# One unit's second product by seven block products for eight, two copies moved to ScalarE, one group of products in two steps, and a new hand-written order

## The chip, the cores and the metric

The kernel runs on one core of one Trainium2 chip. The metric is the device time of one execution in microseconds (us), lower is better. The core's engines work side by side, each through its own queue and in its own order: TensorE (PE in the profile; its weight loads are PEld), VectorE (DVE), ScalarE (ACT), GpSimd (POOL) and SyncE (SP, which here only issues DMAs). All arithmetic is in float32.

## The reference, cut to what matters

`x` is 8 batches x 8 heads x 512 tokens x 64, `state` is 8 x 8 x 32 x 64; `w_in` is 512 x 2048 and `w_out` 2048 x 512, both handed over as float64.

```
a  = softmax(x @ state^T / 8)        # over the 32 states
xread = a @ state
a2 = softmax(state @ x^T / 8)        # over the 512 tokens
sread = a2 @ x
rows = concat([xread, sread]) laid out as (8 * 544) x 512
h = rows @ w_in
out = (h * erf(softplus(h))) @ w_out
```

## The kernel before, in words

**Units.** Attention's result for the tokens of a batch is never formed: `a` (kept as `y`) is multiplied by state @ w_in instead (function `mixed`, steps `A1m`, `A2m` and so on). The hidden dimension is done in two halves, A and B. A *unit* is one batch in one half: A1 to A7, then B0 to B7; SA and SB are the state rows of all batches. The first unit, batch 0 in half A, has a function of its own, `first_unit`, as everything waits for it at the start: its steps are named `n..` (mixed), `h..` (first product and activation) and `o..` (second product).

**Products by sevens.** All other units form a product of two matrices cut in 2 x 2 blocks from seven block products in place of eight, with sums and differences of blocks made by VectorE before (Strassen-Winograd). `hidden` does so for the first product (steps `A1f01` to `A1f17`, matmuls at line 704); `second` (line 767) does it once for a second product (steps `..p1` to `..p7` with four matmuls of 128 x 256 for each half, line 757), `second_twice` does it within each of the seven again (line 827). The four differences of `w_out` that they need are the steps `T1` to `T4`, VectorE, 128 x 1024 each.

**The first unit.** `first_unit` (line 967) makes eight hidden blocks k = 0 to 7: two steps of matmuls (`hkL`, `hkR`, line 987), softplus by ScalarE (`hks`), a copy of h by VectorE (`hkc`, line 1000), erf for two blocks at a time by ScalarE (`h0e`, `h2e`, `h4e`, `h6e`) and the product with h by VectorE (`h0g` to `h6g`). The second product is plain: for each of four row blocks, eight matmuls of 128 x 512 into one PSUM bank (line 1009, 16 steps `o00` to `o36` of two matmuls each), then one copy by ScalarE (`o0c`) and one store (`o0d`). Its steps lie scattered among those of A1 and A2.

**What sets the order.** Every piece of work is a named step. The string `ORDER` (lines 23 to 179) is a hand-written list of all 2,532 step names; `in_order` (line 1149) chains each engine's instructions in just that order, so no engine ever takes a later step while an earlier one waits. `~7*3` stands for three matmuls that compute nothing, which keep TensorE running.

**The start.** The tokens of batch 0 are turned on TensorE (`x00` to `x31`), then come scores in two parts (`t0`, `t1`), and for each part VectorE and ScalarE do the softmax: `max`, `less`, `exp`, `sum`, `inv`, `norm` (line 244), TensorE turns the result (`ta0`, `ta1`), and ScalarE copies it to `y` (`ta0c`, `ta1c`), which `h0L` and `h1L` read. Meanwhile the float64 words of `w_in` and `w_out` arrive in pieces and are converted: `i0a0`, `i0a1` on ScalarE, `i0v0` and `i0v1` on VectorE or GpSimd (lines 379 to 385), and likewise for `i1` to `o3`. `a1..` and `a2..` are the attention of the next batches, mostly on VectorE.

**ScalarE's tables.** Softplus, exp and erf are in different function tables here; the compiler puts a table load ahead of the first instruction that needs another one. The built program has 60.

Of the kernel before, what the change touches and what calls it, by code (L numbers as in the profile page):

```python
# [23 lines left out]
warm lx1 own lx2 lst0 lx3 lx0 i0l0 i0l1 i1l1 i1l0 i2l1 x10 s0 x10c x30 s0c0 x11 x30c s0c1 x20 x00  # L24
x20c x31 i2l0 x00c x21 x31c t0 s0c i0a0 x11c i3l1 i0a1 i0v0 i0v1 i0+a0 x01 i3l0 max0 x21c x01c
i0+a1 less0 ~7*2 t1 i0+v0 ls1 exp0 i0+v1 sum0 i1a0 o0l1 n00 max1 o0l0 q0 i1a1 inv0 q1 less1 norm0
exp1 n01 a1xq6 i1v0 q1c ~7*1 ta0 n01c0 sum1 a1xq7 n01c1 ta0c inv1 n00c1 n00c0 norm1 i2a0 ~7*3 h1L
i1v1 ta1 i2a1 i2v0 h0L ta1c q0c i2v1 i3a1 n02 big1 ub h0R a1xq3 n02c1 i3a0 big0 h1R a1xq2 ubc
n02c0 big i3v0 wt0 n10 h1c a1xq0 h3L i3v1 wt1 n10c1 h2L o1l1 o0a0 h0c a1xq5 a1tx3 h3R n10c0 o0a1
a1xq1 wz h2R wn0 n12 wn1 a1xq4 h5L n12c1 y01 h3s tw1 o1l0 o0v0 n12c0 o3l0 h0s y02 tw0 h2c o3l1 h1s  # L30
o2l1 tw1c h3c h5R o2l0 tw0c a1tx1 o0v1 h2s h6L h5c rd0 a1tx2 a1tx0 h0e h7L rn0 y04 h2e h0g rt0 yl0
h7R a1x3 rc0 o1a0 h6R h2g a1s o1a1 o1v0 h6c h4L o1v1 a1c1 a2xq7 h7c a1c0 h4R a1my1 a2xq5 o00 a1tu0
a1tu1 h7s hold a2xq6 a1mx0 h5s lst7 A1m h6s a1mx1 a1x2 lst2 a1sb0 lst1 a1sb1 lst3 a1x0 a1ex0 o20
a1my0 lst6 a2xq3 a1ex1 a1sm0 lst5 A1m11 a1sm1 A1m10 lst8 o02 A1m00 a1iz A1M1 A1m01 lst4 a2xq0 o2a1
a1nm0 o22 a1nm1 o2a0 a2xq4 a1ta0 a1ta1 a1ey0 A1f01 t0k y11 A1M2 A1f05 A1f0c y12 y13 a1ey1 A1f06
a1ty0 o3a0 a1ty1 A1f02 A1M3 a1kz A1f0u2 u0 y14 a2xq2 o3a1 A1M4 A1f07 a1iy a1x1 o3v0 A1f0c11 u1
A1f0u3 u0c o3v1 A1f11 a2xq1 A1f0c22 A1f04 u1c h4c h4s A1f03 A1f0c21 t01 A1f0s22 o10 T1 A1f1c a1z0
a1z2 t02 a1z3 o2v0 A1f16 a1z1 yk1 h4e A1f0c12 o2v1 A1f12 yl1 a2tx2 t3k A1f1u2 A1f15 h6e a2tx0
A1f17 A1f1c11 o12 T2 A1f1u3 t61 A1f1c22 rd1 A1f0s21 t41 A1f0s11 h4g A1f14 rn11 a2x0 rn10 rt1 y03
A1f13 h6g rc1 A1f1s11 a2s A1f0s12 T4 o04 a2c1 a3xq4 t21 a2c0 A1f1c12 A1f1c21 a3xq3 a2tu0 A1f1s22  # L40
o14 a3xq1 A1f1s21 t31 A1f1s12 a2mx0 a3xq6 o24 yk0 a2my0 a2sb0 a3xq5 A1e0 o26 a3xq2 A1e1 A1g0 o06
a3xq0 t1k a3xq7 o16 A1g1 a2x3 a2ex0 A2m a2ey0 a2sm0 o0c a2ey1 o0d o30 t32 t4k A2m10 a2iz a3tx0
a2x2 a2nm0 A2m11 A2m00 o32 a3tx2 A2M1 o34 a2ta0 a2ty1 A2f01 y21 a2ty0 o36 A2f0c A2M2 a2kz A2m01
y22 t2k t11 a2x1 A2f06 y24 A2M3 A2f02 t12 A2f0u2 y23 o3c A1q A2f05 A2f0c11 o2c A2f07 A2M4 A1ap50
t04 A2f0u3 T3 A2f11 a2z0 a2z3 A2f0c22 A2f04 a2z1 a2iy a2z2 A1A1 A1ap10 yl2 A2f0c21 o2d A2f1c A2f03
t22 o3d t42 o1c A1A2 A2f16 o1d t5k A2f12 t51 A2f1u2 A1A4 A1ap11 A2f0c12 A2f17 A2f0s22 t33 A2f1c11
rd2 t23 t13 A2f1u3 t34 A2f1s11 t52 A2f14 A1A3 rn20 rn21 A2f0s21 rt2 A1ap51 rc2 A1a2 A1ac A2f0s11
a3s t62 A1a3 A1ap60 a3c1 a4xq6 a3c0 A1ap61 A1b2 a3x1 a4xq1 A1ap20 t03 A1au2 t44 A2f0s12 a3tu0
a4xq2 A2f15 A1ap70 t14 a3mx0 a4xq0 A1ap71 t6k A2f1c22 A1ap21 a3sb0 A1au3 a4xq3 a3my0 A2f13 A1ac11
A1ap40 A1ac22 A1a4 A1bp10 a3ex0 A1bp11 t24 a3ey0 A1ap30 a3sm0 A2f1c21 A1ap41 a3ey1 a3iz A2f1c12  # L50
a3nm0 A1ap31 a4tx0 A3m A2f1s12 A1ac12 A1ac21 t43 A1bc a3ta0 A1d2 A1bp50 A1d3 A3m00 a3x3 A3m10
A1bp60 y31 A2f1s21 a3ty0 A1bp61 t53 A1bp51 A1b3 A1bu2 A3f01 A3m11 t63 A3m01 A1bp20 a3ty1 A2f1s22
A3M1 A3f0c a3kz A1bp70 t64 a4xq4 A3M3 A1bp71 A1bp21 y32 a3x2 t54 A2e0 A3f05 A1b4+ A3M2 A3f02 A1b4
a3x0 A3f06 A1bu3 y34 a4xq7 y33 A1bc22 A1bp40 A3f0u2 A2g0 A2e1 A1bp41 a3z3 A3f07 a3z0 a3z2 A1bp30
a3z1 A3f0u3 A3M4 A1d0 A3f0c11 A1bp31 yk2 A3f0c22 A3f04 a4xq5 A1bc12 A3f11 A2g1 A3f0c21 A1bc11
A3f03 A1bc21 A3f1c A1d1 A2ap10 A2q A3f16 A3f0s11 A1D0 rd3 a3iy A3f0c12 A3f1u2 A2A1 A3f17 rn31 a4x1
rn30 A3f0s12 a4x0 rt3 a4tx2 A3f0s21 A3f15 rc3 A3f1u3 A2ap50 A1D1 A2A2 A3f14 yl3 A3f1c22 A3f12 A2A4
A3f1c21 A2ap11 A3f1c11 A2a2 a4s A2ac A3f1s11 A2A3 A2ap20 a4c1 a5xq4 a4c0 A1U2 A2ap60 a5xq3 a4tu0
A1D4 A2ap61 a5xq2 A2a3 A3f13 A2au2 a5xq0 A3f1s22 A2ap21 A2b2 A3f0s22 a4x2 A2ap70 a5xq1 A2ac11
a4mx0 A3f1s12 A2ap71 a5xq6 A3f1c12 a4sb0 A2ap51 A2au3 a4my0 A3f1s21 A2bp10 A2bp11 A2a4 A2ap40  # L60
a4ey1 a5xq5 A2ap41 A1U3 a4ex0 A2b3 A1D2 A4m a4ey0 A2ac22 A1D3 A2ac21 a4sm0 A2bc A2ap30 A4m11 a4iy
a4iz A4m00 a5tx0 A2ap31 a4nm0 A4m10 A2bp60 A2ac12 A2bp61 A3e0 A2bp50 A4M1 a4ta0 A2bp51 A2bp20
A2b4+ y41 A2bp21 a4ty0 A4f01 A2bu2 A4m01 y42 A4M2 A2bp70 A4f0c a4ty1 A3e1 A2bp71 y44 A4f06 a4kz
y43 A2d3 A2b4 A4f05 a5xq7 A4M3 A2bu3 A4f0u2 A4f02 A2bc22 A2d0 A3g0 yl4 A2bp30 A4f0c11 A2bc11 A4f07
# [122 lines left out]
def kernel(  # L187
# [8 lines left out]
    nc = tc.nc  # L196
# [3 lines left out]
    P = 128  # L200
# [994 lines left out]
```

## Time and profile before

| | us |
|---|---|
| three runs: median (lowest to highest) | 682.49 (682.04 to 684.77) |
| the profiled execution, its own time | 681.77 |
| the profiled execution, span from first to last instruction | 680.0 |
| TensorE busy in the span | 673.0 |
| VectorE busy | 582.7 |
| ScalarE busy | 483.7 |
| granted TensorE clock, mean | 1.000 of full |

A float32 matmul of 128 x 128 x N is recorded as two instructions, so counts at lines 704, 757, 827 and 1009 are twice the number of matmuls. The duration of one instruction in the records overlaps with the next one's; what one more instruction costs its engine is the distance from start to start. By the waits of TensorE, it was held up four times by a named wait in the whole span, for 3.0 us in total, all before 35 us:

```profile
PE b L444 <- DMA big<-in_x_dram: 1.1, 2, 0.8
PE b L456 <- ACT big L250: 0.8, 1, 0.8
PE b L431 <- PEq L1179: 0.8, 1, 0.8
PE b L549 <- DVE sn L250: 0.3, 1, 0.3
```

### The profile page before, as it was taken

How to read it: one execution, taken by the hardware profiler on the slowest of the kernel's cores; microseconds unless marked ns; L12 is line 12 of the kernel's file. 1: busy time of each engine (PE TensorE's matmuls, PEld its weight loads, DVE VectorE, ACT ScalarE, POOL GpSimd, SP SyncE). 2: the span in 40 equal slices, each digit the busy share in tenths (PEclk: the TensorE clock that was granted, in tenths of full speed). 3: DMA queues.
4: the chain of work that ended last, by engine and by line, in shares of the span. 5: the costliest groups of instructions: out<-in, count | busy, mean ns of one | idle time of the engine just before them, and what ended most of it. 6: DMA issues, size and time to landing. Idle time of an engine off the chain costs nothing.

```text
span 680.0 us, 13845 instructions
## 1 busy us (share of the span) xinstructions
PE 673.0 (99%) x5578; PEld 589.3 (87%) x5578; DVE 582.7 (86%) x763; ACT 483.7 (71%) x758; POOL 125.1 (18%) x103
## 2 busy tenths in 40 slices
PE   8999999999999999999999999999999999999997
PEld 7756488988888898999998889899989898989996
DVE  5999899999989999998896689897966797878795
ACT  5998867877695877766886975767595768575831
POOL 0442202122232214020201013011111110201122
PEclk9999999999999999999999999999999999999999
DMA  9896753896796885784966355133232224141347
GB/s 296 199 271 182 154 163 78 215 165 159 148 189 127 186 213 102 209 191 119 224 214 163 87 129 100 26 59 60 32 79 38 43 30 116 20 67 17 46 89 123
DMA packets 145840, 87.16 MB, mean 128 GB/s; under 512 B 92784, under 2 KB 138096, under 8 KB 145776
## 3 DMA queue, kind: packets, MB, share of 16 engines
q1 hardware_dynamic: 126720, 67.78, 36.1%
q0 software_dynamic: 18512, 17.96, 21.1%
q8 instruction: 44, 0.72, 0.4%
q10 hardware_dynamic: 544, 0.52, 0.2%
q14 instruction: 20, 0.16, 0.1%
HBM read 46.14 MB, written 40.11 MB: 127 GB/s over the span
## 4 chain that ended last, share of the span: by engine, by line
PE 97%; DMA 1%; ACT 1%; issue 0%; SPq 0%; DVE 0%; ACTq 0%; DVEq 0%
PE b L827 47%; PE b L704 26%; PE b L1009 4%; PE b L655 4%; PE b L1049 4%; PE b L757 4%; PE b L987 2%; PE b L925 2%; PE b L539 1%; DMA big<-in_moe_w_in_dram 1%; PE b L564 1%; PE b L976 0%; PE b L456 0%; PE b L469 0%; PE b L463 0%
## 5 line engine op out<-in xcount | busy, mean ns | idle before, releaser
L735 POOL DMA_DIRECT2D out_dram<-res x67 | 80.0, 1337 | 425.9 <-DVE res L242 193.9
L827 PE MATMUL b<-big,ring 128*128 128x128 f32 x1196 | 150.3, 276 | 0.0
L827 PEld LDWEIGHTS b<-big,ring 128*128 128x128 f32 x1196 | 144.4, 192 | 6.7 <-issue 2.5
L250 ACT COPY ring<-b 128x512 f32<-128x512 f32 (+1 forms) x136 | 78.1, 584 | 89.5 <-PE b L704 69.4
L704 PE MATMUL b<-y,m 128*128 128x256 f32 x480 | 122.0, 381 | 0.1
L250 ACT COPY res<-b 128x512 f32<-128x512 f32 (+2 forms) x126 | 64.7, 521 | 47.8 <-PE b L827 38.3
L704 PEld LDWEIGHTS b<-y,m 128*128 128x128 f32 x480 | 86.2, 191 | 11.0 <-issue 1.0
L704 PE MATMUL b<-sy,m 128*128 128x256 f32 x360 | 91.4, 381 | 0.0
L244 DVE TENSOR_TENSOR ring<-ring 128x2048 f32<-128x2048 f32 (+1 forms) x36 | 77.6, 2168 | 8.2 <-ACT ring L712 6.1
L693 ACT ACTIVATE ring<-ring 128x512 f32<-128x512 f32 x128 | 77.9, 634 | 2.2 <-DVE ring L242 1.7
L704 PEld LDWEIGHTS b<-sy,m 128*128 128x128 f32 x360 | 65.3, 190 | 9.2 <-ACT b L250 0.8
L827 PEld LDWEIGHTS b<-ta,ring 128*128 128x128 f32 x548 | 68.0, 192 | 5.3 <-ACT b L250 1.7
L827 PE MATMUL b<-ta,ring 128*128 128x128 f32 x548 | 72.3, 276 | 0.0
L242 DVE TENSOR_TENSOR ring<-ring,b 128x512 f32<-128x512 f32 (+1 forms) x72 | 47.3, 660 | 28.5 <-PE b L704 15.7
L243 DVE TENSOR_TENSOR ring<-ring 128x1024 f32<-128x1024 f32 (+3 forms) x66 | 70.5, 1073 | 0.2
L827 PE MATMUL b<-big,ta 128*128 128x128 f32 x572 | 70.7, 275 | 0.0
L827 PEld LDWEIGHTS b<-big,ta 128*128 128x128 f32 x572 | 67.8, 192 | 1.3 <-ACT b L250 0.8
L242 DVE TENSOR_TENSOR res<-res,b 128x512 f32<-128x512 f32 (+2 forms) x60 | 36.1, 601 | 29.8 <-PE b L827 17.6
L712 ACT ACTIVATE ring<-ring 128x2048 f32<-128x2048 f32 x30 | 57.2, 1912 | 0.2
L250 ACT COPY b<-b 128x512 f32<-128x512 f32 (+2 forms) x63 | 34.6, 551 | 23.7 <-PE b L704 10.8
L242 DVE TENSOR_TENSOR res<-res 128x512 f32<-128x512 f32 (+1 forms) x56 | 42.1, 753 | 1.7 <-ACT res L250 0.8
L242 DVE TENSOR_TENSOR ring<-ring 128x1024 f32<-128x1024 f32 (+1 forms) x35 | 39.8, 1142 | 0.2
(153 smaller groups left out, 989.8 us busy)
## 6 DMA issues: line engine op xcount, KB each, us to landing
out_dram<-res POOLq DMA_DIRECT2D x63, 256.0 KB, 5.5
out_dram<-res SPq DMA_DIRECT2D x32, 256.0 KB, 3.4
big<-in_x_dram SPq DMA_DIRECT2D x30, 256.0 KB, 4.8
big<-in_x_dram SPq DMA_DIRECT2D x112, 64.0 KB, 3.1
big<-in_moe_w_in_dram SPq DMA_DIRECT2D x12, 512.0 KB, 7.1
big<-in_moe_w_out_dram SPq DMA_DIRECT2D x12, 512.0 KB, 4.7
kept_y<-y SPq DMA_DIRECT2D x8, 512.0 KB, 3.9
y<-kept_y SPq DMA_DIRECT2D x8, 512.0 KB, 4.3
```

Of the source, the lines that this page charges most:

```text
L242: add = lambda o, a, b: tt(o, a, b, op=ALU.add)
L243: sub = lambda o, a, b: tt(o, a, b, op=ALU.subtract)
L244: mul = lambda o, a, b: tt(o, a, b, op=ALU.mult)
L250: do[name] = lambda: f(*args)
L655: pe.matmul(out=to[j][e][q, :], lhsT=by, rhs=w_in[r, 4 * j:4 * j + 4, i, :], start=True, stop=True)
L693: act.activation(out=o, in_=i, func=ACTF.Softplus)
L704: pe.matmul(out=to[:, i], lhsT=xs[n - 1][:, q:q + P], rhs=ys[n - 1], start=(start and i == 0), stop=(i == 1), skip_group_check=True)
L712: step(u + "e%d" % o, lambda s=s: act.activation(out=s, in_=s, func=ACTF.Erf))
L735: nc.gpsimd.dma_start(out=to, in_=of, accum_op=ALU.add)
L757: pe.matmul(out=to[:, E2 * h:E2 * h + E2], lhsT=a[:, k // 2, k % 2], rhs=rhs[n][:, k], start=(start and h == 0 and k == 0), stop=(k == 3), ...
L827: pe.matmul(out=out_[:, P * j:P * j + P], lhsT=lhs[:, i], rhs=rhs[:, i], start=(start and j == 0 and i == 0), stop=(i == 1), skip_group_ch ...
L1009: pe.matmul(out=bank[3 + r % 3], lhsT=s[:, k, P * r:P * r + P], rhs=wo[0].w[:, k, :], start=(k == 0), stop=(k == NT - 1))
```

## The change

1. The second product of the first unit is done by `second`, now called A0: seven block products of 2 x 4 matmuls of 128 x 256 (56 in all) in place of 32 of 128 x 512. VectorE makes four sums of its blocks (`A0A1` to `A0A4`, 128 x 1024 each); ScalarE takes five results out of PSUM (`A0pc`, `A0pu2`, `A0pc11`, `A0pu3`, `A0pc21`) and VectorE two (`A0pc22`, `A0pc12`), where ScalarE took four. Four stores of the same size go out, cut by quarters and not by rows. `T1` to `T4` must now come before this product's parts, not after the plain product's last read of `w_out`.
2. The copies `h6c` and `h7c` go from VectorE to ScalarE.
3. `A1m` (line 649) becomes `A1m0` and `A1m1`, eight matmuls of 128 x 512 each.
4. `ORDER` is new from its start to about two thirds of its length; its last 783 names, from `B0ap30` on, are the same. Fillers of nothing in the start go from six matmuls to eleven. The compiled program now has 63 table loads, three more: one net in the work of A1 and A2, two in that of A7. Up to the copy `A1f0u2` (the second result that product A1 takes out of PSUM) it has six, where it had five.

```diff
-        def product():
-            for j in range(2):
+        def product(*js):
+            for j in js:
...
-        step(u + "m", product)
+        if u == "A1":
+            for j in range(2):
+                step("A1m%d" % j, product, j)
+        else:
+            step(u + "m", product, 0, 1)
...
-    def second(u, w, slot, nh, store):
+    def second(u, w, lhs, nh, store):
...
-                step("h%dc" % k, dve.tensor_copy, hs[:, k], to)
+                step("h%dc" % k, act.copy if k > 5 else dve.tensor_copy, hs[:, k], to)
...
-        def product(r, ks):
-            for k in ks:
-                pe.matmul(out=bank[3 + r % 3], lhsT=s[:, k, P * r:P * r + P],
-                          rhs=wo[0].w[:, k, :], start=(k == 0), stop=(k == NT - 1))
...
+        (A11, A12), (A21, A22) = ([s[:, 4 * k:4 * k + 4, 256 * r:256 * r + 256] for k in range(2)]
+                                  for r in range(2))
+        S1, S2, S3, S4 = (hs[:, 4 * (k // 2):4 * (k // 2) + 4, 256 * (k % 2):256 * (k % 2) + 256]
+                          for k in range(4))
+        step("A0A1", add, S1, A21, A22)
+        step("A0A2", sub, S2, S1, A11)
+        step("A0A3", sub, S3, A11, A21)
+        step("A0A4", sub, S4, A12, S2)
+        xs = (A11, A12, S4, A22, S1, S2, S3)
+        return lambda n, h, k: xs[n - 1][:, k, P * h:P * h + P]
...
-    seconds0()
     for n, f in enumerate(wo[0].sums()):
         step("T%d" % (n + 1), f)
+    second("A0", wo[0], lhs0, 2, lambda r, c, of: put(
+        rows_of(0)[:, 2 * r:2 * r + 2, E2 * c:E2 * c + E2],
+        of.rearrange("p (h e) -> p h e", h=2), False))
```

The new order around the start and the first unit (of the changed kernel; `...` leaves out names):

```
... x31 x11c x31c x21 x11c i0+a0 t0 i3l1 i0+a1 i0+v0 x21c i0+v1 i0a1 i3l0 t1 i0a0 max0 i0v0 less0
ls1 o0l1 i0v1 q0 exp0 max1 i1a0 q1 sum0 n00 i1a1 less1 a1xq2 inv0 i1v0 ~7*3 n01 n00c0 o0l0 exp1
norm0 i2a0 sum1 a1xq3 ~7*5 ta0 n00c1 q1c inv1 norm1 n01c0 ta0c i2v0 i2a1 ~7*3 ta1 i1v1 h0L ta1c ...
n02 ub h0R ... h1L ... h1R ...
... yl0 A1m0 a1mx0 h6s a2xq0 hold a1sb1 lst1 A0p10 ... A0p11 h7c ... A1m1 h6c ... A1f01 y11 ...
A1f07 ... A1f17 rn11 a2x3 rn10 t0k rt1 T2 A0p20 rc1 A0A1 ... A0p50 ... A0p60 ... A0d2
```

More of the change, by code (lines that the diff above doesn't have):

```diff
@@ L23 @@
 ORDER = """
[L24 to L52, printed above, removed]
@@ new lines @@
+s0c1 x20 x10c x31 i2l0 x20c x11 x31c x21 x11c i0+a0 t0 i3l1 i0+a1 i0+v0 x21c i0+v1 i0a1 i3l0 t1
+i0a0 max0 i0v0 less0 ls1 o0l1 i0v1 q0 exp0 max1 i1a0 q1 sum0 n00 i1a1 less1 a1xq2 inv0 i1v0 ~7*3
+n01 n00c0 o0l0 exp1 norm0 i2a0 sum1 a1xq3 ~7*5 ta0 n00c1 q1c inv1 norm1 n01c0 ta0c i2v0 i2a1 ~7*3
+ta1 i1v1 h0L ta1c n01c1 i2v1 i3a0 a1xq5 q0c n02 ub h0R big0 i3a1 big1 h1L a1xq7 ubc n02c0 big i3v0
+n10 wt1 a1xq4 n02c1 h1R i3v1 wt0 h0c h3L o1l0 o0a0 n10c1 h1c a1xq0 h2L a1tx1 n10c0 a1xq6 h2R wz
+wn1 n12 wn0 h1s a1xq1 h3R o0a1 n12c1 y01 o1l1 tw1 y02 n12c0 o3l0 o0v0 h2s tw0 o2l1 h0s h2c o0v1
@@ new lines @@
+o3l1 tw1c h4L h3c o2l0 tw0c a1tx2 h3s rd0 a1tx3 a1tx0 h4R a1x1 rn0 h0e y04 rt0 t01 h7L h4c rc0
+o1a0 h0g a1s h2e o1v0 h6L a2xq6 a1c1 h2g h5L o1a1 h7R a1tu1 a2xq7 a1c0 o1v1 a1my1 h6R a1tu0 h5R
+a1x0 a1mx1 h7s yl0 A1m0 a1mx0 h6s a2xq0 hold a1sb1 lst1 A0p10 a1sb0 a1x2 a1ex1 a1my0 lst5 a1ex0
+a1sm1 a2xq5 lst3 A0p11 h7c a1sm0 a1ey1 lst6 a2xq4 a1iz A1m00 lst2 a1nm0 A1m1 h6c lst8 a1nm1 a1ey0
+lst7 a1ta0 o2a0 lst4 a1ta1 A1f01 y11 A1m11 a1ty1 A1m10 a1ty0 A1m01 A1M1 A1f0c a1kz o3a0 y12 a2xq1
+A1f05 A1M2 o2v0 a2xq3 A1f06 A1M3 A1f02 y13 h5s a2xq2 T1 A1f0u2 u1 A1f0c11 A1f07 a1x3 A1M4 o3a1 y14
@@ new lines @@
+A1f11 a1z0 o3v0 A1f0u3 a1z1 a1z3 h5c o2a1 o3v1 A1f04 a1z2 A1f0c22 u0 h4s u1c A1f0c21 a2tx2 A1f03
+A1f1c o2v1 u0c A1f12 A1f0c12 A1f16 a2tx0 h6e A1f15 h4e a1iy h6g rd1 A1f1u2 A0pc h4g A1f17 rn11
+a2x3 rn10 t0k rt1 T2 A0p20 rc1 A0A1 A1f0s22 a2s T3 A1f1u3 A0p50 a2c1 a3xq5 A0A2 a2c0 A1f0s12 a2x0
+A0A3 a3xq2 A1f14 A1f0s11 A1f0s21 A0p60 a3xq4 a2tu0 y03 A1e0 a3xq1 a2mx0 A0p61 a3xq6 A1f1c22 a2sb0
+A0p21 a2my0 yk0 A0pu2 t1k a3xq7 A1f13 T4 yl1 a2ex0 a2x1 A0p70 A0A4 a2ey1 t6k a3xq3 A1f1c21 a2sm0
+A0p71 A0pc11 t31 t03 a2iz A0p51 a2x2 A1f1c12 A0pu3 a2nm0 A0d0 A1f1c11 a3tx2 a2ey0 A2m A0pc22 t02
@@ new lines @@
+t32 A1f1s22 a2ta0 A0p40 A2m01 A2m00 t11 a2ty1 A2m10 a2ty0 A2m11 A2f01 A1f1s11 A2M1 a2kz A0p30
+A1f1s12 y21 a3xq0 A2f0c t21 y22 A1f1s21 A2M3 A2f02 A2M2 A2f05 y24 A1e1 y23 A1g0 A2f06 A0p31 A2f0u2
+A2f0c11 a2z1 A1g1 a2z3 A2f07 a2z0 a2z2 A1ap10 A2f0u3 yk2 t2k A2f11 A2M4 yl2 A2f0c22 A0d3 A2f04 A1q
+A0p41 A2f0c21 a2iy A2f1c A1A1 A2f16 a3tx0 rd2 A2f1u2 A0pc12 A2f17 A1A3 rn21 a3x2 rn20 A0d1 rt2
+A2f12 A2f1u3 t3k t23 A0pc21 t5k A1A2 A2f14 rc2 A0d2 A1ap11 t34 t13 t12 a3s A1ac A1a2 A2f03 a3c1
+a4xq6 t22 A1a3 a3c0 A1ap20 a4xq4 A1ap21 a3tu0 a4xq3 A1ap60 A1ac11 t33 a4xq0 a3mx0 A2f1c11 A1ap50
@@ new lines @@
+a4xq2 A1ap61 A2f0c12 a3sb0 a4xq1 a3my0 A2f15 A1au2 yk1 A1bp10 A2f1c22 t4k a3x0 t14 A1ap70 a3ex0
+t24 a4xq5 t04 A1ap71 A1A4 a3ey1 A2f13 a3ey0 a3sm0 A1ap51 A1au3 a3x3 A2f1c21 t51 A1bp11 a3x1 t41
+A1ap40 a3iz A2f1c12 a3nm0 A1ac22 A1ap41 A2f0s12 a4tx0 A2f1s22 A3m A1ac21 A1a4 A1bc A2f0s11 A2f1s11
+A1bp20 t61 t52 A3m11 t62 A1bp21 A3m01 t42 A1ap30 A3m10 a3ta0 A1bc11 A1ap31 A3m00 A1b2 A2f1s21
+A3f01 A2f0s21 a3ty0 A1bp60 A1ac12 A3f0c A2f1s12 t43 A1bp61 A1d0 t53 A1bp50 a3ty1 A1bu2 A2f0s22 y31
+A1bp51 a3kz A1b3 A3f02 A3M1 A1bp70 A2e0 t63 y32 A3f05 A3M2 t54 A1bp71 y33 A3f06 A1D0 t44 A1bu3
@@ L1005, in first_unit @@
                 step("h%dg" % k, mul, s[:, k:k + 2], s[:, k:k + 2], hs[:, k:k + 2])
-        def product(r, ks):
-            for k in ks:
-                pe.matmul(out=bank[3 + r % 3], lhsT=s[:, k, P * r:P * r + P],
-                          rhs=wo[0].w[:, k, :], start=(k == 0), stop=(k == NT - 1))
-        def seconds():
-            for rs in (0, 1, 2), (3,):
-                for k in range(0, NT, 2):
-                    for r in rs:
-                        step("o%d%d" % (r, k), product, r, (k, k + 1))
-                for r in rs:
-                    step("o%dc" % r, act.copy, res[:, r], bank[3 + r % 3])
-                    step("o%dd" % r, lambda r=r: nc.sync.dma_start(
-                        out=rows_of(0)[:, r, :], in_=res[:, r]))
-        return seconds
+        (A11, A12), (A21, A22) = ([s[:, 4 * k:4 * k + 4, 256 * r:256 * r + 256] for k in range(2)]
[8 more added lines that the diff above has]
+        return lambda n, h, k: xs[n - 1][:, k, P * h:P * h + P]
     def states_y():
@@ L1120 @@
         if b < TWICE:
-            second("A%d" % b, wo[0], b % 2, 2, store)
+            second("A%d" % b, wo[0], in_ring(b % 2, 2), 2, store)
         else:
```

276 lines of the change are left out of this document (139 added, 137 removed).

## The prediction

> **What bounds it now.** I read the page first: busy shares, the slices, the chain that ended last.
>
> ```profile
> PE 673.0 (99%) x5578; PEld 589.3 (87%) x5578; DVE 582.7 (86%) x763; ACT 483.7 (71%) x758; POOL 125.1 (18%) x103
> ...
> PE   8999999999999999999999999999999999999997
> ...
> DVE  5999899999989999998896689897966797878795
> ACT  5998867877695877766886975767595768575831
> ...
> PE 97%; DMA 1%; ACT 1%; issue 0%; SPq 0%; DVE 0%; ACTq 0%; DVEq 0%
> ```
>
> TensorE never rests after the first slice (17 us), and the chain of waits is TensorE at 97%. So taking work off TensorE should pay in full, unless another engine is as late. The DVE row warns of that: it stands at 9 through the first half. Next I asked for busy time in windows of 20 us (columns: stretch, length, PE, PEld, DVE, ACT, POOL, clock, DMA share, GB/s).
>
> ```profile
> 30.00:50.00 20.00, 19.66 (x167) 11.04 (x166) 19.37 (x35) 19.38 (x29) 9.35 (x11) 1.00 1.03 258
> 50.00:70.00 20.00, 19.90 (x149) 12.87 (x148) 19.27 (x30) 18.18 (x31) 4.80 (x2) 1.00 0.59 163
> 70.00:90.00 20.00, 20.00 (x82) 9.62 (x81) 18.48 (x25) 13.85 (x21) 3.82 (x2) 1.00 0.71 167
> 90.00:110.00 20.00, 20.00 (x201) 17.46 (x201) 19.66 (x31) 12.35 (x24) 1.49 (x1) 1.00 0.50 134
> ```
>
> From 30 to 110 us VectorE is idle for 3.2 us of 80, and from 30 to 70 ScalarE for 2.4 of 40. The first unit's second product lies exactly there (39 to 88 us). Three engines are full at once, so TensorE's saving counts only as far as the other two can follow.
>
> **TensorE's work.** The chain in order of time shows what a step of each kind costs:
>
> ```profile
> 42.76 5.35 PE b L1009 x12
> ...
> 364.52 1.73 PE b L757 x8
> ```
>
> A plain product's instruction (line 1009) costs 5.35/12 = 0.446 us; 32 matmuls are 64 instructions, 28.5 us. A block product's (line 757) costs 1.73/8 = 0.216; 56 matmuls are 112 instructions, 24.2 us. **-4.3 us**, on the path if nothing else is late. A1m in two steps issues the same matmuls; it adds one switch from narrow to full tiles, 0.1 to 0.2 us (L704 x8 takes 1.92 or 1.93 behind such groups, else 1.73). Five more fillers stand where TensorE waits anyway; nothing.
>
> **The start: +1.1 us.** I followed the softmax of batch 0 in the timeline.
>
> ```profile
> 15.58 0.68 DVE L244 TENSOR_TENSOR ring<-ring,z 128x512 f32<-128x512 f32 x1
> ...
> 17.06 0.58 ACT L250 COPY y<-b 128x512 f32<-128x512 f32 x1
> ...
> 17.80 1.10 PE L987 MATMUL b<-y,m 128*128 128x256 f32 x4
> 18.81 0.66 PE L469 MATMUL b<-ident,ring 128*128 128x128 f32 x4
> 19.30 1.03 PE L987 MATMUL b<-y,m 128*128 128x256 f32 x4
> 20.26 0.66 PE L976 MATMUL b<-w_in,st 64*32 64x256 f32 x16
> ```
>
> These are norm0, its copy ta0c, h1L, ta1, h0L and n02. The three loads ahead of the first piece of w_in are the same three, reordered, so I let it land as before (first conversion at 9.10, second piece at 10.58). In the new order i0v0 stands before less0 on VectorE and waits for i0a0, which ScalarE finishes at 10.60 + 0.59 + 0.67 = 11.87, 0.2 us after max0. i1v0 (0.61) too now comes before norm0. From less0 at 12.25, VectorE does i0v1, max1, sum0, less1 (0.60 each), inv0 (0.38) and i1v0: norm0 at 16.25, not 15.58. ScalarE's copy ta0c stands behind i2a0, q1c and n01c0 and runs from 18.25 to 18.84, 1.2 us later than in before. norm1 comes at 18.05 (18.08 before), so ta1 at 18.85 and h0L at 19.4: the same time, but without the 0.86 us of h1L, which before has done by then. n02 waits for i1v1, 16.85 + sum1, n00c1, inv1, norm1, i2v0, i1v1 = 20.5 (20.26 before). 0.86 + 0.25 = 1.1. Bounds: 0 if the first piece lands earlier, +2 if later by 1 us.
>
> **From 20 to 62 us: +3.0 us of new waits.** Two checks, one for each full engine.
>
> ScalarE, from ta0c to A1f0u2, the copy that A1f07 waits for. The listed work is equal in both orders, 31.3 and 31.4 us from start to start: h6c and h7c (0.96) and a table load (1.29) come in, while o2a1 goes behind that point and i2a0 ahead of ta0c (1.9; i2a0 is in ta0c's lateness already). In before's trace this work took from 17.64 to 51.88:
>
> ```profile
> 38.64 1.28 ACT L693 ACT_TABLE_LOAD   x1
> ...
> 51.32 0.56 ACT L250 COPY ring<-b 128x512 f32<-128x512 f32 x1
> ...
> 51.93 1.13 PE L704 MATMUL b<-y,m 128*128 128x256 f32 x4
> 60.76 1.06 PE L704 MATMUL b<-y,m 128*128 128x256 f32 x4
> 61.65 1.88 PE L1009 MATMUL b<-ta,ring 128*128 128x512 f32 x4
> ```
>
> that is 34.2 us, of which some 1 us idle. From 18.84 that gives 52.1 without idle time, 53.1 with as much. So A1f07 starts at 52.2 to 53.1, not 51.93 (third line), although TensorE has less to do before it.
>
> VectorE, from i1v1 to h4g, on which step A0p20 waits. Its list there is 39.3 us: of 128x1024 five at 1.13 and two turns at 1.15; of 128x512 ten sums and eight reductions at 0.60, ten turns at 0.62, seven copies at 0.60; five conversions at 0.60; the rest small. As a control, the same sum for before from i1v1 to a1ta0 is 25.6 us, and the trace took 27.8: 2.2 more, most of it idle. Going through the new list I find 0.1 to 0.5 at h2c, h2g and a few others, 2 us with the hand-offs. 20.5 + 39.3 + 2 = 61.8.
>
> TensorE's own work until there, from before's rows: from n02 to 61.65 (after A1f17, last lines) are 41.4 us, less five plain steps (8.9), plus h1L (0.86), rd1 and rt1 (1.36), A0p10 and A0p11 (3.45), the switch (0.15): 38.3. From 20.5 it would be there at 58.8. It gets there at 61.8, having waited **3.0 us**, mostly at A1f01 (a1ta0), A1f05 (A1M1), A1f07, A1f12. Queued behind each of these are all of TensorE's later steps. Bounds: 0, if all idle time of both engines goes; 5, if ScalarE idles as in before and the 2 us become 4.
>
> **After 62 us: 0.** From A0p20 to A2f15 TensorE has 44.0 us of steps and some 0.6 of switches, VectorE from h4g to A2f0c12, which A2f15 waits for, 43.1 with A0A1 to A0A4 (4.5) in it. Its margin is 1.5 us, and I find 0.5 idle (A2M1 behind the copies A2m10 and A2m11). So A0's sums are covered by A0's own products; without that margin they cost up to 2 us (a rival). The three extra loads of ScalarE (windows: 6 to 8 us free of 20 between 70 and 110 us) and the copies are covered by that free time. The stores: four as before, SyncE issues them behind loads that are not waited for. From B0ap30 on nothing changes.
>
> The Trainium skill, "ScalarE: Activation LUTs", section "What ACT_TABLE_LOAD costs", gives a switch of tables a load of 1283 ns and a drain of some 1380 ns. The trace has the load (1283 ns) but no drain: the next instruction starts 0.01 us behind it, and from the end of the one before it is 1.3 us. By the page the extra load before A1f0u2 would cost 1.4 us more, and the sum would be +1.2; the row decides against it.
>
> **Sum.** -4.3 + 1.1 + 3.0 + 0 = -0.2 us on the profiled execution's 681.77 (680.0 of span and 1.8 around it): 681.6. The median shown is 0.7 above that execution, so 682.3.
>
> **Rivals.** (a) *TensorE alone counts*: the waits of 20 to 62 us don't come, since VectorE and ScalarE lose idle time when the order fits them; for it speaks that before's waits after 35 us are none. Then -4.3 + 1.1 = -3.2, and -4.3 if the start is as before: 678.2 to 679.3. Against it: 39.3 us of VectorE can't go into the 38.3 of TensorE, and ScalarE's equal work starts later.
> (b) *VectorE stays behind*: the four sums and the early T1 to T4 make it late after 62 us. It decides from the point where its idle time between 62 and 130 us is over 1.5 us; before had 3.5 from 50 to 130 (windows). Then +2.0, and with 3 us more, where DMA-fed turns of the next batch (a2tx, a3tx) come late, +5: 684.3 to 687.3, slower than before.
> (c) *The page's drain*: +1.2, 683.7, inside no change.
> (d) *The change doesn't do what it says*: the built program has 56 matmuls of 128x256 more and the 32 of 128x512 are gone, so no chance.
>
> **How the numbers follow.** Forecast (-2 to +1.5) 0.50, (a) 0.22, (b) 0.25, (c) 0.03. A difference of 0.5% (3.4 us) is about what a measurement of this kernel can tell from no change. Faster by more needs under 679.1: over half of (a), 0.14. Slower by more needs over 685.9: half of (b), 0.13. The rest, 0.73, is within. The range from 679.0 to 685.8 reaches into (a) and (b) and leaves out 0.2.
>
> **What would show it.** Right: the line 757 group grows to 112 instructions more at 0.216 and line 1009 is gone; n02 near 20.5; A1f07 at 52 to 53 with waits of TensorE for DVE and ACT of 2 to 4 us in total between 40 and 62; A0p20 near 62; few waits after. Wrong: waits under 1 us (then faster, a), or TensorE waiting for VectorE at A2f or A1a steps from 80 to 150 us (then slower, b); or the first conversions far from 9.1 us.

## The result, and the profile after

| | before | changed |
|---|---|---|
| median of 20 executions each, us | 682.44 | 684.11 |
| profiled execution, own time / span, us | 681.77 / 680.0 | 683.23 / 681.4 |
| executions with a mean TensorE clock of 0.999 or 1.000, of all whose clock is on record: number, median | 83 of 105, 682.54 | 20 of 32, 683.03 |
| executions with a lower mean clock: number, median | 22 of 105, 683.46 | 12 of 32, 685.28 |

Executions with a mean clock of 0.999 or 1.000 are called undisturbed from here on.

The ratio is 1.0022 (95% interval 1.0013 to 1.0031): slower by 1.5 us, within half a percent. A second comparison (e5) gave 1.0006 (0.9987 to 1.0024). The forecast was 682.3, 0.2 us below before, in a range of 679.0 to 685.8: the time lies in the range, but it moved the other way.

The two profiled executions, from which the following is read, differ by 1.46 us, but the undisturbed medians by only 0.5 (by 0.2 in e5's comparison, 683.0 for 682.8). Before's profiled execution was a fast one, 0.8 us under its undisturbed median; that of the changed kernel lies 0.2 us above its own.

The changed kernel's page, the rows that answer to those of before:

```profile
PE 671.6 (99%) x5636; PEld 600.1 (88%) x5636; DVE 585.2 (86%) x767; ACT 489.3 (72%) x764; POOL 125.3 (18%) x103
...
PE   9889999999999999999999999999999999999997
...
DVE  5899999999999999988995689897966797878795
ACT  5999957778596867875877975767585768575831
...
PE 92%; ACT 3%; DMA 2%; SPq 2%; issue 0%; DVE 0%
```

TensorE works 1.4 us less than before (671.6 for 673.0), and the span is 1.4 us longer: so it stands still 2.8 us more. In the slices its row shows 8 in the second and third slice, where before had 9. The chain that ended last is no longer TensorE at 97% but at 92%: 3% of it is ScalarE, 2% DMAs and 2% SyncE's queue. The windows of the prediction, once more:

```profile
30.00:50.00 20.00, 17.23 (x170) 11.36 (x168) 18.93 (x33) 19.36 (x32) 9.59 (x11) 1.00 1.01 257
50.00:70.00 20.00, 19.39 (x157) 14.77 (x158) 19.97 (x29) 19.19 (x29) 4.77 (x2) 1.00 0.59 133
70.00:90.00 20.00, 20.00 (x116) 16.20 (x115) 19.17 (x30) 18.29 (x27) 3.83 (x2) 1.00 0.73 183
```

Between 30 and 50 us TensorE (first number after the comma) has 17.23 us of 20, where it had 19.66; VectorE (the third) is still nearly full, 18.93. Behind 70 us TensorE never rests. The waits of TensorE by their releasers (us in total, times, longest):

```profile
PE b L709 <- DVE m L243: 1.5, 1, 1.5
PE b L550 <- DVE sn L251: 0.9, 1, 0.9
PE b L1081 <- DMA st<-in_state_dram: 0.8, 1, 0.8
...
PE b L709 <- DVE y L251: 0.5, 1, 0.5
```

The largest is step A1f05, for the sum A1M1 of VectorE. VectorE starts that sum at 49.59 us, straight behind its step before; ScalarE ends the last copy that the sum needs at 49.55. So the two engines are equally late there, which is why the chain can go through ScalarE and have 0% of VectorE. Where A1f05 stands is seen in the timeline of TensorE:

```profile
46.15 1.09 PE L656 MATMUL b<-w_in,st 64*32 64x512 f32 x16
47.70 1.10 PE L709 MATMUL b<-y,m 128*128 128x256 f32 x4 [0.46 <-DVE y L251]
50.29 2.13 PE L709 MATMUL b<-sy,m 128*128 128x256 f32 x8 [1.49 <-DVE m L243]
```

These are A1m1, A1f01 and A1f05. In before, A1f01 and A1f05 (with A1f06 in the same row) had no wait:

```profile
47.95 1.03 PE L704 MATMUL b<-y,m 128*128 128x256 f32 x4
48.81 2.01 PE L704 MATMUL b<-sy,m 128*128 128x256 f32 x8
```

Following named steps through both traces, A1f05 starts 1.48 us later than before (50.29 for 48.81), and the last steps of the kernel 1.42 us later (B7p30 at 667.31 for 665.89). So between these two executions **everything is decided ahead of A1f05**. Some of the 1.48 us is what executions differ by: in e14, whose order is before's up to 81 us, A1f05 started at 49.38. Behind it both kernels have twelve steps of the first unit's second product left (21.1 us of plain steps, 21.2 us of block products), and all else is the same work. Ahead of it before had four plain steps (7.1 us), the changed kernel has two steps of A0 (3.7 us): the whole saving of 3.4 us lies there, in front of a place where TensorE waits for VectorE.

### The profile page after: what moved, and what is told of

It reads as the page before. It is cut to its first block, busy times and chain, and to the rows that moved or that the text cites. A ratio compares the mean times of both kernels' runs of the same rounds, so it can differ in the third digit from the quotient of the medians.

```text
span 681.4 us, 13976 instructions
## 1 busy us (share of the span) xinstructions
PE 671.6 (99%) x5636; PEld 600.1 (88%) x5636; DVE 585.2 (86%) x767; ACT 489.3 (72%) x764; POOL 125.3 (18%) x103
## 4 chain that ended last, share of the span: by engine, by line
PE 92%; ACT 3%; DMA 2%; SPq 2%; issue 0%; DVE 0%
PE b L837 47%; PE b L709 26%; PE b L767 7%; PE b L656 4%; PE b L1054 4%; PE b L935 2%; DMA st<-in_state_dram 1%; SPq L395 1%; PE b L540 1%; PE b L997 1%; PE b L565 1%; ACT ta L380 0%; DMA big<-in_x_dram 0%; ACT ring L251 0%; ACT L698 0%
## 5 line engine op out<-in xcount | busy, mean ns | idle before, releaser
L244 DVE TENSOR_TENSOR ring<-ring 128x1024 f32<-128x1024 f32 (+3 forms) x69 | 74.1, 1085 | 0.1
```

Of the source, the lines that this page charges most:

```text
L244: sub = lambda o, a, b: tt(o, a, b, op=ALU.subtract)
```

## The experiments

All are the changed kernel with the edit shown, unless they are said to be the kernel before. Names that only move within the order are shown as a diff of the order.

**e1: a wait of the start taken away.**

```diff
-i3l1 ... i3l0 t1 i0a0 max0 i0v0 less0 ls1
+ls1 i3l1 ... i3l0 t1 i0a0 max0 i0v0 less0
```

> The changed kernel with one move: the load of batch 1's state, which step ub waited 0.84 us for, is issued ahead of the last two pieces of w_in instead of behind them. Theory W (VectorE and ScalarE have no idle time between 34 and 63 us, and VectorE is held at 33.7 us by the tokens of batch 1): TensorE is 0.8 us earlier from 21 to 31 us, but the waits at rt0, A1f01 and A1f05 grow by as much, A0p20 still starts at 62.9 to 63.2, and the time is within 0.3 us of the changed kernel's (683.8 to 684.4). Rival T (TensorE's own time counts, a wait removed is a gain): 0.8 us less, 683.3.

684.11 (ratio 1.0019, 1.0002 to 1.0037), undisturbed 683.26. The wait at ub is gone (ub at 20.64 us, not 21.39), and yet A0p20 came 0.8 us later (63.91). In this execution the last token load was late (a1tx0, the turn of these tokens on VectorE, at 34.53, for 33.74 in the changed kernel), and A1f01 came at 48.50. Rival T has no support: TensorE was earlier at 20 us and not at 50, and the undisturbed executions are not shorter (683.26 for 683.03). Whether moving the state's load made the tokens late was not tried.

**e2: VectorE relieved by GpSimd.** T1, y14 and A1M4 by `nc.gpsimd.tensor_tensor`, each also earlier in the order (T1 ahead of A1f01).

```diff
-        step("y%d4" % b, sub, T4, Y21, T2)
+        step("y%d4" % b, psub if b == 1 else sub, T4, Y21, T2)
-        step(u + "M4", sub, S4m, X12, S2m)
+        step(u + "M4", psub if u == "A1" else sub, S4m, X12, S2m)
```

> The changed kernel with three VectorE steps given to GpSimd, which is free there: T1 (1.22 us), A1M4 (0.65) and y14 (0.38), all between 50 and 56 us and before h4g, on which A0p20 waits. Theory W1 (VectorE's list alone sets A0p20): A0p20 1.2 to 2.2 us earlier, time 681.9 to 682.9. Rival W2 (ScalarE is as full: h4g starts 0.23 us behind h4e, which ScalarE ends at 61.45): A0p20 at most 0.3 us earlier, time 683.8 to 684.2. Against both: if GpSimd slows VectorE beside it, slower than 684.4.

688.40 (1.0079, 1.0065 to 1.0093), against both theories. GpSimd's queue, then VectorE's, in this kernel:

```profile
46.53 2.38 POOL L244 TENSOR_TENSOR ta<-ta 128x1024 f32<-128x1024 f32 x1
```

```profile
45.40 1.30 DVE L427 TENSOR_SCALAR z<-z 128x32 f32<-128x32 f32 x1
...
47.12 2.94 DVE L597 TENSOR_TENSOR big<-big,z 128x512 f32<-128x512 f32 x2
```

Around GpSimd's sum (its recorded spans are rough), VectorE's 128x32 instruction takes 1.30 us (0.18 in the changed kernel) and two of 128x512 take 2.94 (1.29). a1ta0 comes at 49.99, not 46.85, A1f01 waits 4.6 us, and from 50.6 to 57.4 us TensorE has half its clock. The Trainium skill, "SBUF — State Buffer", section "SBUF: two separate sides", says that the two engines share a pair of ports that one of them locks for a whole instruction. The lengths of VectorE's rows fit that; GpSimd's recorded span begins only when the first of them is nearly over (46.53 against 45.40 to 46.70).

**e3: the plain product in the new order.** Plain steps in the places of the seven, two ahead of A1f05 and fourteen behind. T3 now comes after steps that take its place's content for other products, so later products use other numbers; the amount of work is that of the plain product.

```diff
-A0p10 ... A0p11 ... A0p20 ... A0p50 ... A0p60 ... A0p41
+o00 ... o02 ... o10 o20 ... o12 ... o22 ... o34 o36 T3
```

> The changed kernel's order with the plain second product of before in the places of the seven: 32 matmuls of 128 x 512, no sums A0A1 to A0A4, four copies and row stores as before; T3 and A1ap10 come later since they need w_out and a bank of it. Theory W: the order cost its waits before A0p20, the product itself saves TensorE what its steps take less, 28.2 against 24.8 us start to start; so this is 3.4 us slower than the changed kernel, 687.5. Rival R (the four sums of VectorE and the early T1 to T4 eat the saving after 62 us): within 1.5 us of the changed kernel, 684 to 685.6.

691.54 (1.0120, 1.0103 to 1.0137). Up to A1f05 as the changed kernel (50.06 us). Then two more steps cost the expected 3.4 us, and two waits that were not expected, 1.2 and 1.8 us for copies by ScalarE at A2f01 and near 101 us, the rest: 6.5 in all at the end (673.82 for 667.31). Rival R falls. Behind A1f05, in this order, the sevens are worth at least the 3.4 us of the two steps; what the two waits come from was not tried.

**e4: the seven in the old order.** 

```diff
-o00 ... o20 ... o02 ... o22 ... o10 ... o12 ... o04 o14 ... o36
+A0p10 ... A0p11 ... (nothing) ... A0p20 A0p50 ... A0p41 ... A0p30 ... A0p31
```

> The product by sevens alone: the order of before, with its 16 plain steps out; A0p10 and A0p11 at the first two places, nothing at the next four (the other parts of this product need h4g and h6g, which end near 66 us), and the remaining twelve parts from there on; sums behind h6g, h6c and h7c on VectorE as before, A1m in adjoining steps. Theory W: the saving can't be had, since four plain steps that covered the full engines from 42 to 62 us are gone and as much TensorE work comes behind 66 us: TensorE waits 5 to 7 us before h6g, and the time is 2 to 5 us above before's, 684.4 to 687.4. Rival T (TensorE's own time counts): 3.3 us below before, 679.1.

698.13 (1.0206, 1.0181 to 1.0231), far above either. The mechanism of W was there, but not alone: TensorE waited 3.0 us ahead of A1f01 and 3.7 us between 59 and 68 us, and behind 80 us another 7.3 us, where the four sums and T3 had come into VectorE's old list and the next batch was late (that the sums are the cause was not tried by itself; two of the three waits are for copies of ScalarE):

```profile
81.41 1.99 PE L767 MATMUL b<-ta,ring 128*128 128x256 f32 x8 [2.88 <-ACT res L251]
...
93.89 2.05 PE L709 MATMUL b<-y,m 128*128 128x256 f32 x4 [3.23 <-DVE y L251]
```

The third is 1.17 us, at 100.51. Half the clock for 3.4 us behind the first wait of 3.0 and for 6.8 behind that of 3.2 is part of the loss. So the product needs an order of its own; put into the old one like this, it costs 15 us.

**e5: the changed kernel again.** No edit.

> The changed kernel itself, as a control beside the next three. Theory C (a long wait of TensorE is followed by some microseconds at half the granted clock, as the two kernels with waits of 3 and 4.6 us showed; the changed kernel's waits are near that limit, so it happens in some of its executions and not in others): times in two groups, runs of a mean clock of 0.999 or 1.000 at 682.4 to 684, runs of 0.994 to 0.998 at 684 to 688, median near 684.1. Rival (the times scatter for another reason, the clock is a by-product): no gap in time between executions of high and low mean clock.

683.60 (1.0006, 0.9987 to 1.0024). Of twelve executions four are under 0.999, at 684.0 to 687.0 us. With the first twenty: 20 undisturbed at 683.03, ten at 0.996 to 0.998 with 685.12, two at 0.994 and 0.995 with 687.37. The steps of 2.1 and 4.3 us fit the stretches of half clock that the traces show: they were 3.4 us long in e5, in e15 and once in e4, and 6.8 us long in e2, e13, e16 and once in e4, which takes 1.7 or 3.4 us of TensorE's work. In e5's own trace one lies at the start, behind a wait of 1.50 us for tokens (in the windows, TensorE is the first number behind the comma, the granted clock the third from the end):

```profile
6.00:7.40 1.40, 0.00 (x0) 0.00 (x0) 0.04 (x1) 0.82 (x3) 0.00 (x0) 1.00 1.00 334
7.40:10.80 3.40, 3.31 (x16) 3.24 (x17) 1.95 (x5) 2.29 (x5) 0.00 (x0) 0.51 1.06 358
```

n02 came 1.5 us later than in the first trace (21.41), but A1f05 only 0.2 (50.52). In this execution the start wasn't on the path.

**e6: fillers in the waits.**

```diff
-ub ... rt0 ... A1f01 ... A1f05
+~5*3 ub ... ~5*3 rt0 ... ~6*2 A1f01 ... ~6*6 A1f05
```

> The changed kernel with fourteen more fillers of 128 x 128 where TensorE waits: three ahead of ub, three ahead of rt0, two ahead of A1f01, six ahead of A1f05 (each 0.22 us, so 3.1 us of the 3.7 us waited there; nothing is computed by them). Theory C: TensorE is hardly ever idle, the clock stays at 1.000 in all runs, the median falls to 682.5 to 683.2 and the spread to 2 us. Rival W alone (only the waits count, the clock does not): as the changed kernel, 683.8 to 684.4, or above it by what the fillers are too long.

683.62 (1.0006, 0.9992 to 1.0019); all twelve executions at 0.999 or 1.000, spread 2.0 us. Theory C holds for the clock. The median did not fall as far as it said: undisturbed the fillers cost some 0.6 us (683.62 for 683.03), so that nearly all was given back.

**e7 and e8: ScalarE relieved, then VectorE too.**

```diff
-... o3a1 ... o2a1 ... o3v1 ... o2v1 ... T1 ... h4g ...
+... (e7: these four out) ... (e8: and) h4g T1 ...
```

> The changed kernel without the low words of the second half of w_out (o2a1 and o3a1 on ScalarE, 1.05 us each between 53 and 56 us; o2v1 and o3v1 on GpSimd), so w_out loses its last bits there. Theory B (ScalarE and VectorE are equally late before A0p20: h6g starts 0.05 us behind h6e and 0.08 us behind VectorE's own list): A0p20 at most 0.3 us earlier, undisturbed runs within 0.3 us of the changed kernel's. Rival S (ScalarE alone sets it): A0p20 1.5 to 2.1 us earlier, time 1.5 to 2 us less.

> The same, and T1 (VectorE, 1.22 us) moved from ahead of A1M4 to right behind h4g, so that VectorE's list before h4g is shorter too. Theory B: A0p20 1.0 to 1.2 us earlier than in the changed kernel (61.9 to 62.1), undisturbed runs about 1 us less, 681.6 to 682.2. Rival S: no more than the kernel with ScalarE alone relieved. Rival R (VectorE is late behind 62 us, so that T1 there only moves the wait to A0p50 or A0p60): as the kernel with ScalarE alone relieved, with waits of TensorE between 64 and 72 us.

e7 683.32 (1.0008, 0.9990 to 1.0027), e8 684.25 (1.0022, 1.0005 to 1.0039). From A1f01 to A0p20 it took 15.4 us in the changed kernel, 15.3 in e7, 15.1 in e8. So neither S nor B holds: some 3 us less on the two engines buy 0.3. From A1f05 to A0p20 TensorE's own work fills all but 0.3 of the changed kernel's 12.8 us; at A0p20 itself it doesn't wait. e7's execution was 1.3 us early at A1f01, because its tokens were (a1tx0 at 32.02).

**e9: batch 1's tokens first.**

```diff
-h3L o1l0 ... h1s a1xq1
+h3L ... h1s a1xq1 o1l0
```

> The changed kernel with the load of the first piece of o1 (512 KB of w_out) issued behind batch 1's last token loads instead of ahead of the last three. Theory P (the time is set by the chain: last token load, a1tx0, VectorE's unbroken list to a1ta0, A1f01; in all profiles so far A1f01 came 13.9 to 14.5 us behind a1tx0 and A0p20 15.1 to 15.6 behind A1f01, and the rest took the same): a1tx0 starts 0.5 to 0.8 us earlier (33.0 to 33.2 us), as VectorE stands idle 0.77 us for it; A1f01 and A0p20 come earlier by as much; undisturbed runs 0.5 to 0.8 us less than the changed kernel's 683.0. Rival T (TensorE's own start decides, a1tx0 is not on the path): no change of A0p20, 683.0.

683.66 (1.0021, 1.0009 to 1.0034), undisturbed 683.00: no gain in the median. In the profiled execution a1tx0 came 1.8 us earlier (31.91), A1f01 and everything behind it 0.9 us (46.84, and 666.46 at the end). Most of the other 0.9 was lost to the load that was put back: ScalarE waited 0.3 us for o1's piece, VectorE 0.4 and 0.25 behind it. So two loads hold VectorE's list, and shifting one brings up the other. In e11, e12 and e15 (in e11 and e15 with the load in its old place) ScalarE waited 0.9 to 1.4 us for that piece, and A1f01 came at 47.7 to 48.6 whatever a1tx0 did.

**e10 and e11: the sum A1M1 first; and with both engines relieved.**

```diff
-o2a0 ... A1m11 a1ty1 A1m10 a1ty0 A1m01 A1M1 A1f0c
+A1m11 A1m10 A1M1 A1m01 a1ty1 a1ty0 A1f0c o2a0
```

> The changed kernel with A1M1, the sum for which A1f05 waited 1.5 us, ahead of the turns a1ty1 and a1ty0 on VectorE, and the copies A1m11, A1m10, A1m01 it needs ahead of the conversion o2a0 on ScalarE. Theory L (only this place is late): A1f05 1.2 us earlier, A0p20 and the end too, undisturbed runs 681.8. Theory F (VectorE and ScalarE are both full from 34 to 63 us, so an exchange within their lists gains nothing): A1f05 at 49.1, then the wait stands at A1f07 (for A1f0u2, still at 52.9) and A0p20 (for h4g, 62.9), which comes at 63.0 to 63.2; undisturbed runs 682.8 to 683.2.

> The same exchange, with both engines relieved: the conversion of o3 left out (o3a0, o3a1, o3v0, o3v1; its part of w_out is zero), the low words of o2 too (o2a1, o2v1), and T1 behind h4g; ScalarE has 3.2 us less and VectorE 1.8 us less ahead of A0p20. Theory F: now the exchange pays: A1f05 at 49.1, A1f07 at 52.3 to 52.5, A0p20 1.0 to 1.4 us earlier (61.7 to 62.1), undisturbed runs 681.6 to 682.0. Theory L: as with the exchange alone. Rival R (TensorE waits for VectorE behind 62 us instead): A0p20 earlier, the time not.

e10 683.85 (1.0022, 1.0008 to 1.0036), undisturbed 683.77; e11 684.10 (1.0026, 1.0013 to 1.0039). In e10 the wait moved, as theory F said, but to A1f06, for the next sum of VectorE:

```profile
48.33 1.13 PE L709 MATMUL b<-sy,m 128*128 128x256 f32 x4 [0.34 <-DVE m L243]
50.54 1.10 PE L709 MATMUL b<-sy,m 128*128 128x256 f32 x4 [1.08 <-DVE m L244]
```

From A1f01 to A0p20 it took 15.9 us, 0.5 more than unchanged. In e11 it took 15.25: the relief that theory F wanted gave 0.2 us, not 1.0. In both, ScalarE had done its copies 1.7 us and more before VectorE began A1M2, the sum for A1f06 (49.71 in e10, 51.42 in e11), and VectorE worked without a gap from a1ta0 on. So what holds TensorE here is VectorE's row of turns and sums from a1ta0 to A1M2; the total lengths of the lists up to h4g don't.

**e12: tokens first, and five fillers at A1f05.**

```diff
-A1f05
+~6*5 A1f05
```

> The token loads first as in e9, and five fillers of 128 x 128 ahead of A1f05 (1.1 of the 1.5 us waited there). Theory C (the wait at A1f05, when a late start makes it longer, brings the clock down): no run with a mean clock under 0.999, median as e9's undisturbed runs, 682.2 to 682.6. Rival C2 (the clock falls at the start, where TensorE waits for tokens of batch 0 in the first 8 us, as in the one profile that shows it): three to five of twelve runs under 0.999, as in the changed kernel.

685.38 (1.0040, 1.0025 to 1.0056). The clock part holds again (six of six at 0.999 or 1.000), though A1f01 waited 1.54 us in the profiled execution. The time doesn't: TensorE waited 1.6 us near 301 us, for a copy by ScalarE that itself waited 3.0 us for a store, and all six executions are above 684.2. Why five fillers at 49 us bring that about stays open.

**e13 and e14: the kernel before with less work, ahead of A1f05 and behind it.**

```diff
-... o02 o2a1 a1nm0 o22 ...          (e13)
+... o2a1 a1nm0 ...
-... o32 a3tx2 A2M1 o34 ...          (e14)
+... a3tx2 A2M1 ...
```

> The kernel before without two of its plain product's sixteen steps, o02 and o22 (the products of two hidden blocks are left out of two row blocks), which stand ahead of A1f01: 3.5 us less TensorE work at 44 to 48 us. Theory P (up to A1f05 VectorE's list sets the time, so less TensorE work there gains nothing): A1f01 still at 47.7 to 48.0, TensorE waits 3 us and more ahead of it, the clock falls to half for some microseconds as behind the waits of 3.0 and 4.6 us seen so far, and the time is 1 to 3.5 us above before's. Rival T (TensorE's own work counts): 3.5 us below.

> The kernel before without o32 and o34 (two hidden blocks' pairs left out of the last row block), which stand behind A1f05, at 82 to 90 us: 3.4 us less TensorE work there. Theory P (from A1f05 on TensorE's own work is the time) and rival T alike: 3.0 to 3.5 us below before's, 679.2 to 679.7. Against both (VectorE is as late behind 62 us): less than 1.5 us below.

e13 685.12 (1.0025, 1.0010 to 1.0040): 3.4 us of matmuls taken out, and slower. A1f01 came at 49.73 us, not at 47.7 to 48.0 as theory P said, since in this execution VectorE waited 1.5 us for batch 1's tokens (0.35 in before's). TensorE's wait in the timeline, then windows of 2 us (first number behind the comma PE, and third from the end the clock):

```profile
49.73 2.05 PE L704 MATMUL b<-y,m 128*128 128x256 f32 x4 [3.99 <-DVE y L250]
```

```profile
46.00:48.00 2.00, 0.00 (x0) 0.00 (x0) 1.93 (x6) 2.00 (x5) 0.80 (x2) 0.99 0.91 196
48.00:50.00 2.00, 0.27 (x1) 0.30 (x2) 2.00 (x4) 2.00 (x3) 0.00 (x0) 0.50 1.29 239
50.00:52.00 2.00, 2.00 (x6) 1.55 (x6) 2.00 (x6) 0.63 (x3) 0.00 (x0) 0.50 0.85 126
```

Its two undisturbed executions took 682.48 and 682.51, before's on that chip 682.02: what is saved ahead of A1f05 is worth nothing, and if the wait gets long it is worth less than nothing. e14 683.16 (1.0006, 0.9990 to 1.0022), undisturbed 682.04 beside 682.02 of the kernel before on that chip: no gain either, against theory P and rival T. TensorE is idle for 2.9 of the 3.4 us at A2f01, whose y comes from VectorE:

```profile
85.53 1.10 PE L704 MATMUL b<-y,m 128*128 128x256 f32 x4 [2.93 <-DVE y L250]
```

In this execution VectorE was thus no more than 0.5 us ahead of before's TensorE there. The changed order has A2f01 1.6 us earlier (83.75 for 85.31) and no wait. How much room it has was not tried.

**e15 and e16: the wait at A1f05 made longer.**

```diff
+        for k in range(1 if u == "A1" else 0):
+            step(u + "R%d" % k, add, S1m, X21, X22)
         step(u + "M1", add, S1m, X21, X22)
```

> The changed kernel with the sum A1M1 done twice on VectorE (0.6 us more ahead of A1f05), the result is the same: the wait at A1f05 goes from 1.5 to 2.1 us. Theory C (the clock falls behind a wait that is long enough, and costs more than the wait itself): more executions under 0.999 than the changed kernel's four in ten, median 1 to 3 us above its 683.9. Rival (the wait alone counts): 0.6 us above, 684.5, clock as in the changed kernel.

> The same sum done three times: 1.2 us more, the wait 2.7 us. Theory C: nearly all executions under 0.999 with a stretch of some 4 to 7 us at half the clock behind A1f05, median 3 to 5 us above the changed kernel's, 687 to 689. Rival (the wait alone counts): 1.2 us above, 685.1.

e15 685.63 (1.0045, 1.0028 to 1.0062), e16 686.90 (1.0056, 1.0039 to 1.0073): 1.7 and 3.0 us above the changed kernel's pooled 683.9 for 0.6 and 1.2 us more work. All thirteen executions are at 0.994 to 0.998. Theory C holds. e15's row of the wait, and e16's windows (the row names a conversion of ScalarE that ended at 52.01; VectorE's second sum ended at 51.90):

```profile
52.05 1.37 PE L711 MATMUL b<-sy,m 128*128 128x256 f32 x4 [2.31 <-ACT ta L380]
```

```profile
48.00:50.00 2.00, 0.24 (x2) 0.00 (x0) 1.97 (x4) 2.00 (x5) 0.00 (x0) 1.00 1.23 174
50.00:52.00 2.00, 0.72 (x2) 0.66 (x3) 1.97 (x5) 1.97 (x3) 0.00 (x0) 0.59 1.06 306
```

Put together by the wait at A1f05: filled up (0.2 to 0.4 us left) 0 of 18 executions have a low clock; 1.5 us, 12 of 32; 2.3 us, 7 of 7; 3.0 us, 6 of 6.

The traces say more than the length of the wait does. In each of them the clock changes only at whole multiples of 3.41 us from its first record. With the span cut into such cells, half clock followed each of the six cells in which TensorE was idle for 2.2 us or more (2.2 in e13, 2.3 in e15 and in e16, 2.5 and 2.8 in e4, 3.4 in e2). It followed none of the cells at full clock with up to 1.9 us, but for the one of 1.65 us at the start of e5. The waits of 2.93 us in e14 and 2.88 in e4 fell on two cells each (1.1 and 1.9 us, 1.0 and 1.9) and left the clock alone. In the changed kernel the waits at A1f01 and A1f05 make 2.0 us of idle time within 3.1, if one cell holds both. That its low executions lose their clock there is not shown: the only trace of one, e5's, has the stretch at the start.

## Why the prediction was wrong

**The argument held.** TensorE's saving counts only as far as VectorE can follow, and it doesn't follow: the runs of the old order with less TensorE work, ahead of A1f05 (e13) and behind it (e14), gained nothing, and the changed kernel's saving of 3.4 us ahead of A1f05 became for the most part idle time (2.7 us more than before's on TensorE between n02 and A1f05, without the wait at ub). Few waits after 62 us and no change beyond half a percent came as said.

**The step that failed: the term of the product was mis-sized.** "64 instructions, 28.5 us" for the plain product took 5.35/12 from a group whose duration holds the tail of its last matmul, while 1.73/8 for the block product was a distance from start to start. Start to start, and with the switches between shapes of tiles in both, the sixteen plain steps take 28.16 us and the fourteen of A0 24.83: -3.3 us (1.72 for 1.73 us a step, two steps fewer), not -4.3. That alone turns the sign of the sum: -0.2 becomes +0.8.

**The start: +1.1 was +1.4, and not where it was put.** n02 came at 19.88, not 20.5; h1L behind it added its 0.9; and ub waited 0.8 us for the load of batch 1's state, which no part of the sum had. The experiments then showed that the term has no place in a sum: with n02 1.5 us later (e5), A1f05 was 0.2 us later, since VectorE's list and its loads decide there.

**The waits of 20 to 62 us: +3.0 was +3.0, by luck.** TensorE waited 0.2 us at rd0, 0.9 at rt0, 0.5 at A1f01, 1.5 at A1f05 and 0.3 at A1f12, 3.4 in all, of which before has 0.3 at rt0 too. A1f01, A1f05 and A1f12 had been named. A1f07 came at 53.5 (52.2 to 53.1 was said) and A0p20 at 63.1 (61.8), both without a wait of their own. But the reason given, lists of 39.3 and 31.4 us that TensorE must wait out at h4g and A1f0u2, fell with e7, e8 and e11: relieving both engines by up to 3.2 us shortened the way from A1f01 to A0p20 by 0.2 to 0.3 us. The place is narrower: VectorE's steps from a1ta0 to A1M2.

**The switches: 0.1 to 0.2 us were named and then left out of the sum.** A1m in two steps took 2.1 us for 1.9, and A1f01 behind it 1.1 for 0.9; TensorE's own work from n02 to A0p20 was 39.0 us, not 38.3. Over the whole kernel some 0.3 us are left for such things: -3.3 + 1.4 + 3.0 + 0.3 is +1.4, the difference of the two profiled executions.

**Behind 62 us: 0 was right** (1.48 us late at A1f05, 1.42 at the end). Rival (b) didn't come in this order; it did, at 80 to 101 us, when the same product was put into the old one (e4).

**What no case had: the clock.** Of all executions with a clock on record the medians differ by 1.3 us (683.9 for 682.6), of the undisturbed ones by 0.5. The changed kernel has a lower clock in 12 of 32, before in 22 of 105, a difference in number that could still be chance (in e5's comparison 4 of 12 and 7 of 35). What such an execution costs differs more: 2.1 or 4.3 us in the changed kernel, 0.9 in before, where no trace shows the stretch. The profiled clock of before was 1.00, and the wait of 1.5 us was priced at 1.5 us. The Trainium skill, "TensorE: Matmul & The Clock Gate", section "What's actually happening", says that the clock halves after an idle window of 3413 ns that runs freely, and comes back after a busy one. The stretches of 3.4 and 6.8 us and the cells of 3.41 us agree. If it means a window that is idle throughout, that does not: cells with 2.2 to 2.8 us of idle time were enough in e4, e13, e15 and e16, and one with 1.65 in e5.

**Open:** why e12 has a wait near 301 us; how much room VectorE has behind 62 us in the changed order; where the changed kernel's other low executions lose their clock; and what the changed kernel takes on the chips of e9 to e16, where it was not run itself (before's undisturbed median is 682.3 and 682.0 there, 682.8 on e5's). No version here beats before.

## What to carry to other kernels

A saving on a busy engine is worth what it moves at the next place where that engine meets a later one: look where the saved instructions stand in the order, ahead of such a meeting or behind it, before multiplying counts by durations. Take durations from start to start for both sides of a difference. Waits of TensorE that come close together can have a second price, the clock behind them: here half clock followed wherever 2.2 us or more of a cell of 3.41 us were idle. A single profiled execution may not show it; a spread of times beside a spread of mean clocks is its mark, and where the waits were filled it was gone (0 of 18). Before a pair of profiled executions is explained to the tenth of a microsecond, look where each lies among its kernel's times.

## What the runs showed of the hardware

- The granted clock falls to 0.50 for 3.4 or 6.8 us, nothing between, in all six traces that have such a stretch, and changes only on a grid of 3.41 us. Six cells of that grid with 2.2 us or more of idle TensorE brought it down; of those with up to 1.9 us only one did, at the start of e5.
- A sum of 128x1024 by GpSimd takes 2.38 us and holds up VectorE (0.18 us became 1.30, and two sums 2.94 instead of 1.29); its sum A1M4 made A1M3 1.75 us long (0.68). GpSimd's integer sums of the conversions, 2.4 us each, lay beside VectorE's turns and reductions in the changed kernel (38.95 to 41.34 us) without that: 0.70 us and 0.64 each.
- The same load in the same place of the queue landed so differently that a1tx0 started between 32.0 and 33.7 us in kernels whose order is the same up to there (e7 and the changed kernel); undisturbed executions of the changed kernel scatter by 2.8 us (681.97 to 684.79), of which this may be a part.
